# The first pair of attention in a kernel of attention and two expert layers: an early table load, decay pieces on GpSimd, another order of query tiles, and gate weights read at attention's end

## The chip, the cores and the metric

One Trainium2 chip (trn2), one of its cores. The metric is the device time of one execution in microseconds (us), on the one core that runs. Five engines work side by side on a core: TensorE (PE in the rows, with its weight loads as PEld), VectorE (DVE), ScalarE (ACT), GpSimd (POOL) and SyncE (SP). SyncE here only issues transfers; the transfers themselves are carried by 16 DMA engines.

## What is computed

Three operators, one after the other, in float32.

```
attention   q, k, v: 4 x 8 heads x 576 x 64; f: 4 x 8 x 576
            cum    = cumsum(log(clip(f, 1e-4, 1)))
            scores = q k^T / 8 + cum_i - cum_j, causal
            out    = softmax(scores) v
layer 1     x = out as 2304 x 512
            y = (silu(x w_gate) * (x w_val)) w_out        inner width 1536
layer 2     one of 8 experts per row, by argmax(y w_gate) with softmax weight,
            times sigmoid(y w_output_gate); expert: relu(y w1) w2, inner width 1024
```

## The kernel before

**Attention** (class `Attention`) goes through 16 pairs of heads. In a pair the two heads (a = 0, 1) lie in the two halves of the 128 partitions. The 576 queries are cut into five tiles: tile 0 with 64 queries, tiles 1 to 4 with 128 each. `qk(p, i)` makes the scores of tile i of pair p: per head one product q·k into a PSUM tile `ps_s` (four buffers), and one that adds the decay. For tile 4, 576 keys wide, this is done in two halves. VectorE reduces each PSUM tile to its row minimum (L151), ScalarE takes the exponential (L159) into the tiles `e`. The decay term of pair 0 comes from the float32 sums `c8` directly; for the later pairs the sums are split into three bf16 pieces (`decay`, L93 to L96), written to memory (`cd`, L97) and read back as the rows `dk` (L116).

`tr(p, g)` transposes the exponentials on TensorE in four groups g (L175 for the first, L190 and others for the rest); ScalarE and VectorE copy them out of PSUM. `av` multiplies them with v. The row sums are inverted on VectorE (`rb`, L212 and L213), transposed on TensorE (`rt`, L219), copied by ScalarE (L221), written to memory as ten rows of 512 bytes (`rd`, L224) and read back broadcast to 128 partitions x 576 (`rb`, L226). `xout` multiplies the result with that broadcast on GpSimd (L235) and splits it into `xth` and `xtl` (L237, L238). `run` interleaves: the scores of pair p + 1 are made between the transposes of pair p. TensorE's order there is the order of the code (`manual_schedule`); the other engines' order is set by a scheduler, with `issue_after` as a constraint on it. An engine works through its list strictly in order, and so does SP with the transfers.

**SP's queue** carries all these transfers: per pair rd, rb, the load `qk` of pair p + 3 (L108), from pair 2 on in every second pair a weight load for layer 1 (`raw`, L314), the rows `dk` and the load `v` (L113). The constants `cst` (L886, 128 x 474) come once, in pair 1.

**At the start** come f (twice, into both halves), q and k of pair 0, the mask, the identity, v and the next q and k, and, issued by the scheduler ahead of their place in the code, the two gate weights `wg` and `wo` (`Route.gates`, L441, 128 x 4 x 8 each), which VectorE splits into `gw` (L443, L444). The routing uses `gw` while the last sixth of layer 1 runs. `warm` runs matmuls on zeros (`e0[0]`) ahead of the first product.

**Layer 1** (class `MoE1`): `gv` makes two products per step into PSUM tiles `ps_g` (three buffers), each with 12 matmuls (L377). ScalarE takes tanh of the first (L381), VectorE makes `hs` of it (L382, which reads the first product a last time, and L383, the second's), ScalarE and VectorE split it (L384, L385). So a buffer of `ps_g` comes free only when VectorE's L382 or L383 is done. The first matmul of layer 1 stands within pair 15.

Of the kernel before, what the change touches and what calls it, by code (L numbers as in the profile page):

```python
# [9 lines left out]
F32 = mybir.dt.float32  # L10
# [3 lines left out]
ACTF = mybir.ActivationFunctionType  # L14
# [25 lines left out]
class Attention:  # L40
# [32 lines left out]
    def decay_load(self, pool):  # L73
        nc = self.nc
        t = {nm: pool.tile([128, 1024], F32, tag="w", name="dec_" + nm)[:, :S] for nm in ("ft", "cum", "c8")}
        t["pc"] = pool.tile([128, 1024], F32, tag="w", name="dec_pc").bitcast(BF16)[:B * H, :3 * S]
        for a in (0, 64):
            nc.sync.dma_start(out=t["ft"][a:a + B * H], in_=self.io["f"])
            nc.vector.memset(t["ft"][a + B * H:a + 64], 1.0)
        nc.vector.memset(t["c8"], 1.0)  # L80
        return t.values()

    def decay(self, ft, cum, c8, pc):
        nc = self.nc
        pc = pc.rearrange("p (r s) -> p r s", r=3)
        nc.vector.tensor_scalar(ft, ft, 0.0001, 1.0, op0=ALU.max, op1=ALU.min)
        nc.scalar.activation(ft, ft, ACTF.Ln)
        nc.vector.tensor_tensor_scan(cum, c8, ft, 0.0, op0=ALU.mult, op1=ALU.add)
        nc.scalar.activation(ft[:1, :1], ft[:1, :1], ACTF.Exp)
        nc.vector.tensor_scalar_mul(c8, cum, 8.0)  # L90
        self.c8 = c8
        cum, c8 = cum[:B * H], c8[:B * H]
        nc.vector.tensor_copy(pc[:, 0], c8)  # L93
        nc.vector.tensor_sub(cum, c8, pc[:, 0])
        nc.vector.tensor_copy(pc[:, 1], cum)
        nc.vector.tensor_sub(pc[:, 2], cum, pc[:, 1])  # L96
        nc.sync.dma_start(out=self.cd, in_=pc)  # L97

    def warm(self, n):
        z = self.e0[0]  # L100
        tp = self.ps_t.tile([128, 512], F32, name="ps_t")
        for i in range(n):
            self.nc.tensor.matmul(tp[:, :128], z, z, start=True, stop=True)
# [136 lines left out]
    def run(self, extra, pool):  # L240
        dec = self.decay_load(pool)
        self.load(0)
        self.cst.load()
        self.decay(*dec)
        self.vload(0)
        self.load(1)
        self.rows(1)
        with self.tc.issue_after(self.mark[2].ins):
            self.vload(1)
        with self.tc.manual_schedule(engines={PE}):  # L250
            self.warm(WARM0)
            for i in (2, 3, 4, 1, 0):
                self.qk(0, i)
            for p in range(NP):
                with self.tc.issue_after(self.mark[2].ins):
                    if p + 2 < NP:
                        self.load(p + 2)
                    extra[0](p)
                nx = p + 1 < NP
                self.rb(p)  # L260
                exps = None
                for g, qs in enumerate(((2, 3), (4,), (1, 0), ())):
                    self.tr(p, g)
                    if g == 0:
                        self.rt(p)
                    elif g < 3:
                        extra[g](p)
                    if exps:
                        with self.tc.issue_after(self.mark[0].ins):
                            exps()  # L270
                        exps = None
                    if 0 < g < 3:
                        self.av(p, g - 1)
                    if nx:
                        for i in qs:
                            exps = self.qk(p + 1, i, i == 4)
                for g in range(2, 4):
                    self.av(p, g)
                if p + 2 < NP:
                    self.rows(p + 2)  # L280
                    self.vload(p + 2)
                self.xout(p)
# [129 lines left out]
GI = 3  # L412
WARM = (14, 3, 3, 3)
P0, P1 = 1, 1
H0, WARM0 = 2, 10
HALF = (2, 4, 5, 7, 8, 10)


# [475 lines left out]
def tile_kernel(tc, io, out, dbg=None):  # L894
    nc = tc.nc
    with ExitStack() as ctx:
        pool = lambda cx, nm, b=1, **k: cx.enter_context(tc.tile_pool(name=nm, bufs=b, **k))
# [6 lines left out]
        with ExitStack() as c1:  # L904
            xp = pool(c1, "x")
            xth = xp.tile([128, 4, N], F32R, name="xth")
            xtl = xp.tile([128, 4, N], F32R, name="xtl")
            raw = pool(c1, "raw", 2)
            tmp = pool(c1, "dtmp", 1)
            m1 = MoE1(tc, c1, cst, io, wts, raw, tmp, xth, xtl)  # L910
            with ExitStack() as ca:
                cst.attention(pool(ca, "acst"))
                at = Attention(tc, ca, cst, io, xth, xtl)

                todo = []

                def early(p):
                    if p == 1:
                        cst.rest()
                    if p == H0:  # L920
                        todo.extend(m1.parts(0))
                    if p >= H0 and (p - H0) % 2 == 0 and todo:
                        todo[0] = m1.fetch(todo[0][0]), *todo[0][1:]

                dec = []

                def late(p):
                    if p > H0 and (p - H0) % 2 and todo:
                        dec.append(m1.decode(*todo.pop(0), eng=nc.gpsimd))
                        with tc.issue_after(at.mark[0].ins), tc.issue_after(at.mark[1].ins):  # L930
                            next(dec[0])

                def last(p):
                    with tc.issue_after(at.mark[0].ins), tc.issue_after(at.mark[1].ins):
                        if p == H0:
                            cst.split()
                        if dec:
                            for _ in dec.pop():
                                pass

                at.run((early, late, last), wts.pools[0])
            m1.open(c1)
            wab = [wts.pools[0], pool(c1, "wB", 6)]
            slp = pool(c1, "slots", space=PSUM)
            slots = slp.tile([128, 512], F32, name="slots")
            rt = Route(tc, c1, cst, io, per, m1.y)
            rt.gates(pool(c1, "gtmp"))
            CH = [(384 * i, 384) for i in range(6)]
            CL = CH[:4] + [(1536 + 256 * i, 256) for i in range(3)]
            steps = [(g, t0, n) for g in range(6) for t0, n in (CL if g == 5 else CH)]  # L950
            for i in range(len(steps) + 1):
                for f in range(2):
                    if i < len(steps):
                        g, t0, n = steps[i]
                        if g < 5 and t0 == 0 and f == 0:
                            wts.pools = [wab[(g + 1) % 2]]
                            if g:
                                m1.load(g + 1)
                        if i == 1 and f == 0:
                            wts.pools = [wab[1]]  # L960
                            todo.extend(m1.parts(1))
                        if 2 * i + f in HALF:
                            src, hi, lo = todo.pop(0)
                            with tc.issue_after(m1.mark[0].ins), tc.issue_after(m1.mark[1].ins):
                                for _ in m1.decode(m1.fetch(src), hi, lo):
                                    pass
                        if g == 5 and t0 == CH[2][0] and f == 0:
                            wts.pools = [wab[0]]
                            w00 = load_expert(nc, io, wts, raw, 0, 0)
                        m1.gv(g, t0, n, f)  # L970
                    if i:
                        for d in (2 * f, 2 * f + 1):
                            m1.g2(*steps[i - 1], d)
                if i and steps[i - 1][0] == 5:
                    rt.chunk(*steps[i - 1][1:], slots)
            info = rt.finish(slots)
# [89 lines left out]
```

## Time and profile before

| | |
|---|---|
| median of 3 runs | 969.86 us (968.68 to 972.22) |
| the profiled execution | 974.25 us, span 972.4 us |
| TensorE busy | 939.2 us, 97% of the span |
| VectorE, ScalarE, GpSimd busy | 592.1, 412.3, 228.8 us |
| TensorE's mean granted clock | 0.985 |
| attention | the first 209 us of the span |

The span runs from the first instruction to the last; the time of the execution also holds what lies around it. A row of the timeline has the start in us, the duration in us, the engine, the line of the code, the operation, what it writes and reads with the shape, how many instructions the row merges, and in brackets how long the engine was idle before it and what ended that. The granted clock is a share of full speed: 1.00 is 2.4 GHz and 0.50 is 1.2 GHz.

### The profile page before, as it was taken

To read this page: it belongs to the slowest core of one execution; us is meant where nothing else is said; L and a number is where in the kernel's file an instruction comes from. 1 tells how busy PE (TensorE), PEld (TensorE's weight loads), DVE (VectorE), ACT (ScalarE), POOL (GpSimd) and SP (SyncE) were. 2 spreads that over 40 slices of the span, in tenths; PEclk is the share of its full clock that TensorE was granted. 3 is DMA by queue.
4 is the path that set the end of the run, shared out by engine and by line. 5 is a ranking of instruction groups with operands and counts; after the bars stand their busy time and mean duration, and the time that the engine had idled before them with its cause. 6 is when DMAs were issued, how large, how long until landed. Compare 5 with 4: busy or idle time off the path is not lost.

```text
span 972.4 us, 16496 instructions
## 1 busy us (share of the span) xinstructions
PE 939.2 (97%) x6288; PEld 844.3 (87%) x6288; DVE 592.1 (61%) x1420; ACT 412.3 (42%) x903; POOL 228.8 (24%) x205
## 2 busy tenths in 40 slices
PE   8999999799999999999999999999899999999896
PEld 5666565479999999999999999899799999999795
DVE  5677776547487469459458445677785555552731
ACT  5677776534452123123123122333365445542741
POOL 1244444343121011012012000000115354372011
PEclk8999999999999999999999999999799999999998
DMA  5344444322132012013002000111486566582220
GB/s 161 115 134 132 132 131 127 109 66 66 44 109 65 1 45 86 1 32 100 1 22 87 1 1 1 43 56 55 156 284 191 170 217 188 197 296 85 73 91 30
DMA packets 53088, 94.83 MB, mean 98 GB/s; under 512 B 5954, under 2 KB 27086, under 8 KB 53007
## 3 DMA queue, kind: packets, MB, share of 16 engines
q1 hardware_dynamic: 47503, 79.58, 26.8%
q0 software_dynamic: 5504, 14.17, 4.1%
q8 instruction: 50, 0.82, 0.4%
q14 instruction: 31, 0.25, 0.1%
HBM read 84.10 MB, written 10.16 MB: 97 GB/s over the span
## 4 chain that ended last, share of the span: by engine, by line
PE 69%; issue 10%; DVE 8%; DMA 7%; POOL 3%; ACT 2%; SPq 1%; POOLq 0%; DVEq 0%; ACTq 0%
PE ps_g L377 26%; PE ps_y L395 13%; PE m_psy L696 7%; PE m_psg L681 7%; PE ps_s L144 5%; PE ps_t L190 3%; DMA rd<-rt 2%; DMA qk<-qk 2%; DVE dt L327 2%; PE avx L206 2%; PE avy L206 2%; DMA raw<-w 1%; POOL out L722 1%; PE rt_ps L532 1%; ACT e L159 1%
## 5 line engine op out<-in xcount | busy, mean ns | idle before, releaser
L377 PE MATMUL ps_g<-xth,w 128*128 128x384 f32 (+1 forms) x1184 | 308.7, 331 | 0.0
L377 PEld LDWEIGHTS ps_g<-xth,w 128*128 128x128 f32 x1184 | 213.1, 188 | 0.6
L377 PE MATMUL ps_g<-xtl,w 128*128 128x384 f32 (+1 forms) x592 | 196.1, 331 | 0.0
L395 PE MATMUL ps_y<-hh,w 128*128 128x384 f32 (+1 forms) x592 | 160.7, 332 | 2.2 <-DVE y L401 2.2
L681 PE MATMUL m_psg<-ygh,w 128*128 128x304 f32 x512 | 115.3, 307 | 1.2 <-ACT b_o L832 0.8
L696 PE MATMUL m_psy<-h2h,w 128*128 128x304 f32 x512 | 114.6, 306 | 0.0
L377 PEld LDWEIGHTS ps_g<-xtl,w 128*128 128x128 f32 x592 | 111.3, 188 | 0.1
L340 POOL TENSOR_TENSOR w<-ds,w 128x512 fp32r<-128x512 f32 x36 | 49.3, 1369 | 263.6 <-ACT w L339 263.2
L395 PEld LDWEIGHTS ps_y<-hh,w 128*128 128x128 f32 x592 | 107.1, 188 | 4.4 <-DVE y L401 4.1
L159 ACT ACTIVATE e<-e,mx 128x320 f32<-128x320 f32 (+4 forms) x160 | 88.0, 551 | 35.0 <-DVE mx L151 34.4
L608 DVE TENSOR_TENSOR w<-raw,w 128x1024 fp32r<-128x1024 f32 x64 | 76.7, 1222 | 40.8 <-ACT w L607 25.0
L395 PE MATMUL ps_y<-hl,w 128*128 128x384 f32 (+1 forms) x296 | 97.8, 330 | 0.0
L384 ACT ACTIVATE hh<-hs 128x384 fp32r<-128x384 f32 (+1 forms) x74 | 38.2, 516 | 134.4 <-DVE hs L383 134.4
L151 DVE CUSTOM_DVE_ANT_0 e<-ps_s,mask 128x320 f32<-128x320 f32 (+4 forms) x160 | 62.8, 429 | 47.4 <-PE ps_s L144 37.4
L382 DVE SCALAR_TENSOR_TENSOR hs<-hs,ps_g 128x384 f32<-128x384 f32 (+1 forms) x74 | 40.0, 541 | 83.4 <-ACT hs L381 83.4
L681 PEld LDWEIGHTS m_psg<-ygh,w 128*128 128x128 f32 x512 | 85.6, 189 | 1.8 <-ACT b_o L832 1.0
L696 PEld LDWEIGHTS m_psy<-h2h,w 128*128 128x128 f32 x512 | 85.5, 188 | 0.3
L607 ACT ACTIVATE w<-raw 128x1024 fp32r<-128x1024 f32 x64 | 67.4, 1058 | 36.4 <-PE m_psg L681 14.7
L381 ACT ACTIVATE hs<-ps_g 128x384 f32<-128x384 f32 (+1 forms) x74 | 35.5, 479 | 102.2 <-PE ps_g L377 102.1
L401 DVE TENSOR_TENSOR y<-ps_y,y 128x384 f32<-128x384 f32 (+1 forms) x124 | 67.1, 542 | 19.0 <-PE ps_y L395 18.2
L681 PE MATMUL m_psg<-ygl,w 128*128 128x304 f32 x256 | 77.3, 302 | 0.2 <-DVE ygl L649 0.2
L696 PE MATMUL m_psy<-h2l,w 128*128 128x304 f32 x256 | 77.3, 302 | 0.0
(309 smaller groups left out, 1511.6 us busy)
## 6 DMA issues: line engine op xcount, KB each, us to landing
raw<-w SPq DMA_DIRECT2D x64, 512.0 KB
qk<-qk SPq DMA_DIRECT2D x16, 576.0 KB
v<-vL SPq DMA_DIRECT2D x16, 448.0 KB
raw<-mg SPq DMA_DIRECT2D x12, 512.0 KB
raw<-mv SPq DMA_DIRECT2D x12, 512.0 KB
raw<-mo SPq DMA_DIRECT2D x12, 512.0 KB
rb<-rd SPq DMA_DIRECT2D x16, 288.0 KB
yd<-yr SPq DMA_DIRECT2D x18, 256.0 KB
```

The source lines that it names most:

```text
L144: nc.tensor.matmul(ps[a][b:, :n], x, y, start=c == 0, stop=c == 1, tile_position=(h, b))
L151: nc.vector.tensor_tensor_reduce(out=o, in0=x, in1=y, scale=-0.125, scalar=BIGF if prev[a] is None else prev[a][b:], op0=ALU.add, op1=ALU. ...
L159: nc.scalar.activation(es[a][b:, :w], es[a][b:, :w], ACTF.Exp, bias=prev[a][b:], scale=-1.0, accum_out=rs[b:, c:c + 1])
L340: nc.gpsimd.tensor_sub(lo, s3, hi.bitcast(F32))
L377: nc.tensor.matmul(ps[:, :n], w[:, k, fs], x[:, k], start=(k == 0 and c == 0), stop=(k == 3 and c == 2))
L382: nc.vector.scalar_tensor_tensor(s[:, :n], s[:, :n], 1.0, pss[0][:, :n], op0=ALU.add, op1=ALU.mult)
L395: nc.tensor.matmul(ps[:, :n], w[:, f, ds], h[:, f, :n], start=(f == 0 and c == 0), stop=(f == 1 and c == 2))
L401: nc.vector.tensor_add(y, ps[:, :n], y)
L607: nc.scalar.activation(hi, r, ACTF.Copy)
L608: nc.vector.tensor_sub(lo, r, hi.bitcast(F32))
L681: nc.tensor.matmul(ps[:, :C], w[:, k, fs], x[:, k], start=(k == 0 and c == 0), stop=(k == 3 and c == 2))
L696: nc.tensor.matmul(self.P[e][d][:, :C], w[:, f, ds], h[:, f], start=(u == 0 and f == 0 and c == 0), stop=(u == 3 and f == 1 and c == 2))
```

## The change

Five edits. The decay's table load: a one-element `Ln` on a tile of ones stands ahead of everything, so that ScalarE's table load precedes an instruction without a load from memory as its input. The four instructions that make the bf16 pieces go from VectorE to GpSimd. The order of pair 0's query tiles is 3, 4, 2, 1, 0 instead of 2, 3, 4, 1, 0, three matmuls on zeros (`WARM1`) follow them, and `warm` uses `e0[2]` instead of `e0[0]`. For pair 0, `rb` and `rt` stand behind the first two score tiles of pair 1 instead of around its first transposes. The gate weights' reads may be issued only after the last transposes' copy (`mark[1]`) and the last broadcast read (`mark[2]`) of attention.

```diff
@@ decay_load
         t = {nm: pool.tile([128, 1024], F32, tag="w", name="dec_" + nm)[:, :S] for nm in ("ft", "cum", "c8")}
+        one = self.sm.tile([128, 1], F32, name="one")
+        nc.vector.memset(one, 1.0)
+        nc.scalar.activation(one, one, ACTF.Ln)
@@ decay
-        nc.vector.tensor_copy(pc[:, 0], c8)
-        nc.vector.tensor_sub(cum, c8, pc[:, 0])
-        nc.vector.tensor_copy(pc[:, 1], cum)
-        nc.vector.tensor_sub(pc[:, 2], cum, pc[:, 1])
+        nc.gpsimd.tensor_copy(pc[:, 0], c8)
+        nc.gpsimd.tensor_sub(cum, c8, pc[:, 0])
+        nc.gpsimd.tensor_copy(pc[:, 1], cum)
+        nc.gpsimd.tensor_sub(pc[:, 2], cum, pc[:, 1])
         nc.sync.dma_start(out=self.cd, in_=pc)
 
     def warm(self, n):
-        z = self.e0[0]
+        z = self.e0[2]
@@ run
             self.warm(WARM0)
-            for i in (2, 3, 4, 1, 0):
+            for i in (3, 4, 2, 1, 0):
                 self.qk(0, i)
+            self.warm(WARM1)
             for p in range(NP):
...
-                self.rb(p)
+                if p:
+                    self.rb(p)
                 exps = None
                 for g, qs in enumerate(((2, 3), (4,), (1, 0), ())):
                     self.tr(p, g)
-                    if g == 0:
+                    if g == 0 and p:
                         self.rt(p)
...
                         for i in qs:
                             exps = self.qk(p + 1, i, i == 4)
+                    if g + p == 0:
+                        self.rb(p)
+                        self.rt(p)
@@
-H0, WARM0 = 2, 10
+H0, WARM0, WARM1 = 2, 10, 3
@@ tile_kernel
-            rt.gates(pool(c1, "gtmp"))
+            with tc.issue_after(at.mark[1].ins), tc.issue_after(at.mark[2].ins):
+                rt.gates(pool(c1, "gtmp"))
```

The change adds nine lines, so its line numbers are 3 to 9 higher than those of before.

VectorE in the first pair, before: from the scaled decay sums (`dec_c`) to the reduction of the second query tile. `ISA` is the reduction L151; its second row reads the minimum out.

```order
L90 TENSOR_SCALAR dec_c_153<-dec_cum 128x576
L93 CAST dec_pc<-dec_c_153 32x576
L94 TENSOR_TENSOR dec_cum<-dec_c_153,dec_pc 32x576
L151 ISA e,mx<-ps_s,mask 128x5x64
L151 ISA mx 128x1
L95 CAST dec_pc<-dec_cum 32x576
L96 TENSOR_TENSOR dec_pc<-dec_cum,dec_pc 32x576
L443 CAST gw<-gw_2862 128x4x16
L444 TENSOR_TENSOR gw<-gw_2862,gw 128x4x16
L151 ISA e,mx<-ps_s,mask 128x448
```

The same place of VectorE in the change.

```order
L93 TENSOR_SCALAR dec_c_153<-dec_cum 128x576
L154 ISA e,mx<-ps_s,mask 128x448
L154 ISA mx 128x1
L154 ISA e,mx<-ps_s,mask 128x288
L154 ISA e,mx<-ps_s,mask,mx 128x288
L154 ISA e,mx<-ps_s,mask 128x5x64
```

The pieces and the gate weights are gone from between the reductions, and tile 2 (128x5x64) comes after tiles 3 and 4.

SP at the end of attention, before: the writes rd and reads rb of pairs 14 and 15 (rd_97, rd_98) and the weight loads of layer 1.

```order
L224 DMA rd_97<-rt 10x128
L226 DMA rb<-rd_97 128x1x576
L224 DMA rd_98<-rt 10x128
L226 DMA rb<-rd_98 128x1x576
L314 DMA raw<-mv 128x2x512 x2
```

And in the change.

```order
L227 DMA rd_97<-rt 10x128
L229 DMA rb<-rd_97 128x1x576
L227 DMA rd_98<-rt 10x128
L229 DMA rb<-rd_98 128x1x576
L449 DMA gw_2869<-wg 128x4x8
L449 DMA gw_2869<-wo 128x4x8
L322 DMA raw<-mv 128x2x512 x2
```

The two gate reads stand directly behind the last broadcast.

VectorE at the same place, before: from the last copy of attention into layer 1.

```order
L196 COPY ath_2792<-ps_t 128x320
L234 COPY xt<-avy 128x256
L382 SCALAR_TENSOR_TENSOR hs<-hs,ps_g 128x384
L383 SCALAR_TENSOR_TENSOR hs<-hs,ps_g 128x384
L385 TENSOR_TENSOR hl<-hs,hh 128x384
```

And in the change.

```order
L199 COPY ath_2799<-ps_t 128x320
L237 COPY xt<-avy 128x256
L451 CAST gw<-gw_2869 128x4x16
L452 TENSOR_TENSOR gw<-gw_2869,gw 128x4x16
L390 SCALAR_TENSOR_TENSOR hs<-hs,ps_g 128x384
L391 SCALAR_TENSOR_TENSOR hs<-hs,ps_g 128x384
L393 TENSOR_TENSOR hl<-hs,hh 128x384
```

The cast of the gate weights and its subtraction stand between attention's last copy and the first `hs` of layer 1.

## Rows read from the trace of the kernel before

**Rows 1.** Timeline of the first pair, VectorE, ScalarE and TensorE.

```profile
3.20 1.28 ACT L87 ACT_TABLE_LOAD   x1 [3.20 <-DMA dec_ft<-f]
3.24 0.46 DVE L86 TENSOR_SCALAR dec_ft<-dec_ft 128x576 f32<-128x576 f32 x1 [0.35 <-DMA dec_ft<-f]
...
4.49 0.68 ACT L87 ACTIVATE dec_ft<-dec_ft 128x576 f32<-128x576 f32 x1
...
6.60 0.46 DVE L90 TENSOR_SCALAR dec_c<-dec_cum 128x576 f32<-128x576 f32 x1
...
10.92 0.20 DVE L443 CAST gw<-gw 128x64 fp32r<-128x64 f32 x1 [0.74 <-DMA gw<-wo]
...
11.95 0.67 ACT L159 ACTIVATE e<-e,mx 128x448 f32<-128x448 f32 x1 [1.75 <-DVE mx L151]
...
16.09 0.88 PE L175 MATMUL ps_t<-cst,e 128*128 128x128 f32 x4 [1.19 <-ACT e L159]
...
17.87 0.37 PE L219 MATMUL avy<-cst,rr 128*32 128x128 f32 x1 [0.90 <-DVE rr L213]
...
18.17 1.44 PE L144 MATMUL ps_s<-qk 64*128 64x320 f32 x4
...
21.67 1.97 PE L190 MATMUL ps_t<-cst,e 128*128 128x128 f32 x8
```

**Rows 2.** Windows, TensorE: stretch, length, PE busy (instructions), granted clock, DMA share, GB/s.

```profile
17.30:24.10 6.80, 6.23 (x29) 0.50 0.38 97
...
187.50:190.10 2.60, 0.00 (x0) 1.00 0.12 46
191.40:194.80 3.40, 3.40 (x18) 0.50 0.44 114
```

**Rows 3.** Timeline of SP: start, duration of the issue, line, transfer.

```profile
10.21 0.33 SPq L97 DMA_DIRECT2D cd<-dec_pc  x1
12.09 0.34 SPq L116 DMA_DIRECT2D dk<-cd  x1
...
19.80 0.65 SPq L226 DMA_DIRECT2D rb<-rd  x1
...
33.04 0.30 SPq L224 DMA_DIRECT2D rd<-rt  x1
35.02 0.53 SPq L226 DMA_DIRECT2D rb<-rd  x1
...
48.27 0.51 SPq L226 DMA_DIRECT2D rb<-rd  x1
...
60.00 0.51 SPq L226 DMA_DIRECT2D rb<-rd  x1
...
203.76 0.30 SPq L224 DMA_DIRECT2D rd<-rt  x1
211.23 0.51 SPq L226 DMA_DIRECT2D rb<-rd  x1
```

**Rows 4.** Waits of SP up to 222 us: in total, times, longest (us).

```profile
SPq L226 <- DMA rd<-rt: 119.6, 16, 11.6
```

**Rows 5.** Windows, TensorE, while rb(15) runs.

```profile
213.00:219.00 6.00, 6.00 (x36) 1.00 0.12 47
```

**Rows 6.** Instructions of lines L237 and L238 on GpSimd: ns min/median/max.

```profile
L237 POOL CAST xth<-xt x16: 657/664/1166, 33.7 to 221.3; 128x576 fp32r<-128x576 f32 x16
...
L238 POOL TENSOR_TENSOR xtl<-xt,xth x16: 1400/1409/1747, 34.4 to 222.4; 128x576 fp32r<-128x576 f32 x16
```

**Rows 7.** Timeline of the change-over from attention to layer 1.

```profile
209.40 0.42 DVE L234 COPY xt<-avy 128x256 f32<-128x256 f32 x1 [0.92 <-PE avy L206]
209.41 0.44 PE L377 MATMUL ps_g<-xtl,w 128*128 128x384 f32 x1
...
212.20 0.56 DVE L382 SCALAR_TENSOR_TENSOR hs<-hs,ps_g 128x384 f32<-128x384 f32 x1 [2.38 <-ACT hs L381]
...
219.63 1.57 POOL L235 TENSOR_TENSOR xt<-xt,rb 128x576 f32<-128x576 f32 x1 [4.79 <-DVE hl L385]
```

## The prediction

> **What bounds the kernel now.** I read four views, in this order: the timeline of the first pair, the windows with TensorE's granted clock, SP's queue from the first pair to the end of attention, and the timeline of the change-over from attention to the first expert layer. The page's 97% for TensorE says that it bounds the kernel as a whole; it does not say that it bounds attention, and that is what this change needs.
>
> In the first pair the reader is to see three holes. ScalarE's load of the logarithm's table begins only when f has landed, at 3.20, and the logarithm starts at 4.49, although the clamp before it was done at 3.24 + 0.46 = 3.70. VectorE stands 0.74 us at 10.92 for the gate weights, which only the routing uses, and ScalarE, behind it, waits 1.75 us at 11.95 for a row minimum. And TensorE has finished its first transposes at 16.09 + 0.88 = 16.97, yet starts pair 1 at 18.17, because the small transpose L219 waits for VectorE's reciprocal at 17.87 [rows 1]. After these holes the clock falls: from 17.3 to 24.1 it is granted at 0.50, the lower of its two levels (1.2 GHz), and TensorE is busy for 6.23 us of that [rows 2].
>
> In SP's queue the reader is to see who paces the rest of attention. The broadcast rb(p) of pair p is issued when the small write rd(p) has landed. In the first pairs that takes 33.04 to 35.02, in the last 203.76 to 211.23: 7.5 us for ten rows of 512 bytes [rows 3]. All sixteen rb waits are put down to it, 119.6 us together [rows 4]. While rb(15) moves its 288 KB the DMA engines are busy by 0.12 of sixteen, that is about two of them [rows 5]. So rb runs on two engines, and whatever has a share on those two and is issued behind it lands behind it. This loop (rb, the loads behind it, rd, the next rb) takes 13.25 and 11.73 us for pairs 1 to 2 and 2 to 3 [rows 3]. From rb(1) on it, and not TensorE, sets when attention ends: near the end TensorE stands idle from 187.5 to 190.1 for a load that went out in this queue [rows 2].
>
> **The start.** Table load: its own instruction now has no data to wait for, so the logarithm starts at 3.7, a gain of 4.49 − 3.70 = 0.8 at the decay sums. The gate reads leave the start: VectorE loses the 0.74 wait, the 0.20 cast and a subtraction of about the same size. The four decay pieces leave VectorE too. Together they can take away no more than ScalarE's 1.75 us wait, so the last exponentials that the transposes need end earlier by 0.8 to 0.8 + 1.75 = 2.5 us. I take 1.5: tile 4, now second, needs two reductions per half before its exponentials can start, and part of the wait returns there. L219 is moved behind pair 1's first two tiles, which removes the 18.17 − 16.97 = 1.2 us. TensorE so starts pair 1 about 2.7 us earlier, at 15.5, and up to 6.23/2 = 3.1 more is gained if the clock stays at its upper level, which the three added matmuls and the missing holes make likely (70%).
>
> The decay pieces cost nothing: on GpSimd two casts at 0.66 and two subtractions at 1.41 [rows 6] make 4.1 us, from 7.06 − 0.8 = 6.3 [rows 1]; so their write leaves at about 10.8 instead of 10.21 and the read behind it 0.6 later than 12.09 [rows 3]; pair 1 needs them after 15.5. With GpSimd's longest rows (1.17 and 1.75) they would be 1.7 us later still, and still in time.
>
> How much of TensorE's 2.7 to 5.8 us reaches the end? Only what the loop of rb passes on. rb(0) is issued about when it was, 19.8: TensorE is 2.7 earlier, but L219 now stands behind two tiles of pair 1 (18.17 to 21.67 before, at half the clock; half of that, 1.8, at the full one) and its copy behind two exponentials. rb(1) came 35.02 − 19.80 = 15.22 after rb(0), since rd(1) was not ready before 33.04. With TensorE at least 2.0 earlier the loop alone decides: between 11.73 (nothing else in it) and 13.25 (a 512 KB weight load in it); here it carries a 237 KB load of constants, so I take the middle, 12.5. **Gain: 15.22 − 12.5 = 2.7 us**; ends 15.22 − 13.25 = 2.0 and 3.5, and 1.3 if rb(0) is late.
>
> **The end of attention.** The two gate reads now stand behind rb(15) on SP, and on VectorE the cast that waits for them stands right behind the copy of 209.40, ahead of the first layer's first hs [rows 7]. Nobody measured when they land there. The nearest row of a small transfer with nothing ahead is the decay write: 10.21 to 12.09, 1.9 us [rows 3]; issued at 211.23 + 0.51 and 0.5 later, the reads would land at about 214.1. If they have to wait out rb(15), they land just after it, and GpSimd, which waits for rb(15), starts at 219.63 [rows 7] (its row names VectorE's hl, which GpSimd does not read; rb is what it needs): about 219.9. I take the later value, because rd(15), also small and also issued right behind an rb, took 7.5 us and not 1.9.
>
> The Trainium skill's page "DMA: Bandwidth & Descriptors" (section "Queues, rings and completion order") says that each engine consumes its descriptors in ring order and that the completion count of a transfer lands only after that engine's earlier writes; its section "Why a DMA increments its semaphore by 16 and not by 1" says that a 128-partition transfer is spread over all 16 engines and one whose outermost count is 2 over the lowest two. By that rule the sum is the + 4.8 below, by the 1.9 us of a free transfer it would be − 2.7; the rows of rd agree with the rule, and how the gate reads are spread is shown by no row.
>
> What is queued behind the waiting cast: all of VectorE, and hs first, which frees the buffer of the first product. The layer has three such PSUM buffers, of 12 matmuls each; 36 matmuls take 6.0 us [rows 5], from 209.41 to 215.4 [rows 7], when TensorE needs the first buffer back. It gets it when the cast (219.9), the subtraction and hs (0.56) are through: 219.9 + 0.45 + 0.56 = 220.9. **Stall: 5.5 us** (5.2 to 5.8). After an idle stretch of 2.6 us the clock was granted at 0.50 for 3.4 us of work, a loss of 1.7; after the first pair's holes for 6.23, a loss of 3.1 [rows 2]. The new idle stretch is longer than the 2.6, so it falls here too; **2.0 us**, nearer to the first since TensorE then works on without holes. Nothing later takes this back: from here on TensorE is the bound, and the layer's weight loads are released by VectorE's own order and move with it. The order of the stall and of rb(15) is not changed by the gain at the start, since both sides of it move together.
>
> **Sum:** − 2.7 + 5.5 + 2.0 = + 4.8 us. The profiled execution took 974.25 us with a span of 972.4, some 4 us over the median of the runs shown; it should become 979.0. Against the median: 969.86 + 4.8 = **974.7 us**, 0.49% slower.
>
> **Rivals.**
> The gate reads come in time (17%). For it: they are 32 KB, and at the start they delayed VectorE by no more than 0.74 us although much larger loads were ahead of them. Against it: rd. They decide for the stall only if they land after about 214.4, when cast, subtraction and hs would end after 215.4. Then only the start remains: 969.86 − 2.7 = 967.2, faster than before.
> The start's gain is lost (13%): the clock falls in pair 1 as before and rd(0), now behind two tiles at half the clock, makes rb(0) 1.5 to 2.7 us later, so that the loop starts late. Gain 0.5 in place of 2.7: 976.9.
> The loop is not the bound (10%): TensorE's whole gain with the upper clock arrives, 5.8: 969.86 − 5.8 + 7.5 = 971.6. For it: TensorE does not wait for a load in the first hundred microseconds. Against it: the sixteen waits of rows 4.
>
> **The numbers.** The forecast has 60%, its own range 972 to 977.5: the gain between 1.3 and 3.5, the stall between 5.2 and 5.8, the clock's loss between 1 and 3.1. To leave out no more than 2 in 10 the range must reach to the first rival's 967 and to 978: it leaves out half of that rival (8%) and 8% at the other ends. About 0.5%, or 4.85 us, is what a measurement of this kernel can tell from no change. Slower by more: half of the forecast (30%) and most of the second rival (12%), 0.42. Faster by more needs the first rival with more than 4.85 gained: 0.06. Within: 0.52.
>
> **What would show it.** Right: the logarithm near 3.7; pair 1's first matmul near 15.5; rb(0) near 19.8 and rb(1) near 32.3; rb(15) and the end of attention about 2.7 earlier; then a VectorE wait of some 10 us put down to the gate reads, TensorE idle for about 5.5 us after its third product, and 0.50 granted behind it. Wrong: a cast of gw that starts within 3 us of its reads' issue; rb(1) later than 34; an end of attention that moves by 5 us or not at all.

## The result and the profile after

| | before | the change |
|---|---|---|
| median of 5 runs, us | 969.86 (968.11 to 972.22) | 982.09 (978.40 to 984.22) |
| ratio, with its 95% interval | | 1.0109 (1.0087 to 1.0131) |
| profiled execution, us (span) | 974.25 (972.4) | 978.41 (976.6) |
| first product of layer 1 after attention, us | 209.41 | 205.47 |
| TensorE's wait ahead of the fourth product, us | 0 | 7.94 |

The change is 1.1% slower. The forecast was 974.7 us in 967 to 978: the direction was right, the size too small, and the time lies outside the range. The two profiles lie only 4.2 us apart and the medians 12.2; the experiments come back to that difference.

The first pair after the change, in the timeline of VectorE, ScalarE, GpSimd and TensorE (start, duration, engine, line, operation):

```profile
3.79 0.68 ACT L90 ACTIVATE dec_ft<-dec_ft 128x576 f32<-128x576 f32 x1 [1.57 <-DVE dec_ft L89]
...
6.42 0.65 POOL L96 CAST dec_pc<-dec_c 32x576 bf16<-32x576 f32 x1 [3.29 <-DVE dec_c L93]
...
10.21 0.77 ACT L162 ACTIVATE e<-e,mx 128x576 f32<-128x576 f32 x1 [0.52 <-DVE mx L154]
...
13.41 0.88 PE L178 MATMUL ps_t<-cst,e 128*128 128x128 f32 x4 [0.25 <-ACT e L162]
...
14.22 0.81 PE L147 MATMUL ps_s<-qk 64*128 64x320 f32 x4
...
16.04 0.28 PE L222 MATMUL avy<-cst,rr 128*32 128x128 f32 x1
```

The holes of [rows 1] are smaller or gone: the logarithm starts at 3.79 in place of 4.49, ScalarE, once its exponentials have begun, waits 0.52 in place of 1.75, and pair 1 starts at 14.22 in place of 18.17. Its first matmuls take 0.81 us, not 1.44: the clock did not fall.

SP's queue in the timeline, against [rows 3]:

```profile
18.41 0.65 SPq L229 DMA_DIRECT2D rb<-rd  x1
...
31.04 0.53 SPq L229 DMA_DIRECT2D rb<-rd  x1
...
208.50 0.50 SPq L229 DMA_DIRECT2D rb<-rd  x1
209.06 0.48 SPq L449 DMA_DIRECT2D gw<-wg  x1
209.58 0.49 SPq L449 DMA_DIRECT2D gw<-wo  x1
```

And the change-over to layer 1, against [rows 7], in the timeline of GpSimd, VectorE and TensorE:

```profile
217.05 1.40 POOL L238 TENSOR_TENSOR xt<-xt,rb 128x576 f32<-128x576 f32 x1 [4.97 <-DMA rb<-rd]
217.33 1.16 DVE L451 CAST gw<-gw 128x64 fp32r<-128x64 f32 x1 [11.46 <-DMA gw<-wo]
218.51 0.66 POOL L240 CAST xth<-xt 128x576 fp32r<-128x576 f32 x1
218.53 0.72 DVE L452 TENSOR_TENSOR gw<-gw,gw 128x64 fp32r<-128x64 f32 x1
219.17 0.54 DVE L390 SCALAR_TENSOR_TENSOR hs<-hs,ps_g 128x384 f32<-128x384 f32 x1
219.25 1.41 POOL L241 TENSOR_TENSOR xtl<-xt,xth 128x576 fp32r<-128x576 f32 x1
219.77 0.69 PE L385 MATMUL ps_g<-xth,w 128*128 128x384 f32 x1 [7.94 <-DVE hs L390]
```

The gate reads leave 0.56 and 1.08 us behind rb(15) and are there only after it: GpSimd, which waits for rb(15), starts at 217.05, VectorE's cast at 217.33. VectorE has stood for 11.46 us, and `hs`, which frees the first product's buffer, stands behind it. TensorE did its three products and then nothing from 211.83 to 219.77. In the windows behind it (stretch, length, busy time of PE, PEld, DVE, ACT, POOL, granted clock, DMA share, GB/s) the clock has fallen to its lower level (0.5, 1.2 GHz) for 3.3 us, a loss of 1.6:

```profile
211.50:219.70 8.20, 0.33 (x2) 0.01 (x1) 2.33 (x3) 0.00 (x0) 3.09 (x4) 0.78 0.11 30
219.70:223.00 3.30, 3.23 (x10) 3.23 (x11) 1.59 (x4) 0.90 (x2) 0.96 (x1) 0.51 0.00 0
223.00:228.00 5.00, 5.00 (x31) 5.00 (x30) 3.68 (x7) 1.58 (x3) 0.00 (x0) 1.00 0.00 0
```

### The profile page after: what moved, and what is told of

It is laid out like the page before. It is cut to its first block, busy times and chain, and to the rows that moved or that the text cites. A ratio compares the mean times of both kernels' runs of the same rounds, so it can differ in the third digit from the quotient of the medians.

```text
span 976.6 us, 16510 instructions
## 1 busy us (share of the span) xinstructions
PE 936.3 (96%) x6294; PEld 844.5 (86%) x6294; DVE 590.5 (60%) x1417; ACT 411.7 (42%) x904; POOL 232.7 (24%) x209
## 4 chain that ended last, share of the span: by engine, by line
PE 66%; DMA 11%; issue 10%; DVE 7%; POOL 2%; ACT 2%; SPq 0%; POOLq 0%; DVEq 0%; ACTq 0%
PE ps_g L385 25%; PE ps_y L403 13%; PE m_psy L704 7%; PE m_psg L689 6%; PE ps_s L147 5%; DMA rd<-rt 4%; DMA qk<-qk 3%; PE ps_t L193 2%; DVE dt L335 2%; PE avy L209 2%; PE avx L209 1%; DMA dk<-cd 1%; DMA raw<-w 1%; POOL out L730 1%; PE rt_ps L540 1%
## 5 line engine op out<-in xcount | busy, mean ns | idle before, releaser
L403 PE MATMUL ps_y<-hh,w 128*128 128x384 f32 (+1 forms) x592 | 160.8, 333 | 2.2 <-DVE y L409 2.2
L403 PEld LDWEIGHTS ps_y<-hh,w 128*128 128x128 f32 x592 | 107.1, 188 | 4.2 <-DVE y L409 4.0
L162 ACT ACTIVATE e<-e,mx 128x448 f32<-128x448 f32 (+4 forms) x160 | 88.0, 551 | 34.2 <-DVE mx L154 33.8
L403 PE MATMUL ps_y<-hl,w 128*128 128x384 f32 (+1 forms) x296 | 98.0, 331 | 0.0
L154 DVE CUSTOM_DVE_ANT_0 e<-ps_s,mask 128x448 f32<-128x448 f32 (+4 forms) x160 | 62.6, 429 | 46.3 <-PE ps_s L147 37.4
```

Source lines behind the costliest of these rows:

```text
L154: nc.vector.tensor_tensor_reduce(out=o, in0=x, in1=y, scale=-0.125, scalar=BIGF if prev[a] is None else prev[a][b:], op0=ALU.add, op1=ALU. ...
L162: nc.scalar.activation(es[a][b:, :w], es[a][b:, :w], ACTF.Exp, bias=prev[a][b:], scale=-1.0, accum_out=rs[b:, c:c + 1])
L403: nc.tensor.matmul(ps[:, :n], w[:, f, ds], h[:, f, :n], start=(f == 0 and c == 0), stop=(f == 1 and c == 2))
```

## The experiments

**Theory A:** the time is lost at the end of attention, where VectorE's cast waits for reads that stand behind a transfer on two DMA engines. **Rival B:** the edits of the first pair cost it. **Rival C:** the reads are slow by themselves. **Rival D** (of the run with rb in two): rb is bound by its bytes. **Rival E:** the last rows of attention are late, whatever the cast does. The runs fell on chips of two speeds, on which the kernel before takes 969.8 and 983 to 985 us; so only ratios to the kernel before on the same chip are compared, and times inside attention and layer 1. There the chips agree: from the first product to the last matmul of layer 1 the kernel before takes 478.99 us in its first profile, on the faster chip, and 478.95 in two on the slower.

**The change again, and one part undone or done alone.** `again` is the changed kernel. `gates_back` undoes the gate edit, `gates_only` does it alone in the kernel before:

```
 gates_back (in the changed kernel), gates_only has the reverse
-            with tc.issue_after(at.mark[1].ins), tc.issue_after(at.mark[2].ins):
-                rt.gates(pool(c1, "gtmp"))
+            rt.gates(pool(c1, "gtmp"))
```

> The changed kernel once more, unaltered, for a second profile. Theory A (the time is made at the end of attention: the gate reads stand behind rb(15), which runs on two DMA engines, and VectorE and TensorE wait for them) expects the ratio to stay near 1.01, the cast of gw some 8 to 9 us after its reads' issue, TensorE idle 7 to 9 us ahead of its fourth product, and, where this run is slower than the first profile's 978.4, the difference either in that idle stretch or in stretches at the lower clock. Rival B (the edits of the first pair cost the time, the first profile having been a lucky one) expects pair 1's first matmul, rb(0) or rb(1) later than 14.2, 18.4 and 31.0 in a slower run.

> The changed kernel with the gate reads back at their old place at the start; everything else of the change stays. Theory A expects the stall and the cold stretch behind it gone and the gain of the start left: rb(15) 2 to 3 us earlier than the 211.2 of before, the first product of layer 1 some 4 us earlier than 209.4, nothing idle ahead of the fourth product, ratio 0.994 to 0.998 (964 to 968). Rival B expects a ratio of 1.003 or more.

> The kernel before with the gate reads alone moved to the end of attention. Theory A: rb(15) near 211.2, reads behind it, cast of gw near 220 and, if it is as slow as in the changed kernel (1.2 us, with a subtraction of 0.7), the fourth product at 222.3 in place of 215.4: stall 6.9 and 1.5 at the lower clock, together +8.4, ratio 1.007 to 1.010. Rival B expects 1.000 to 1.004. Rival C (the reads are slow by themselves: 1024 rows of 32 bytes) gives the same time here and is told apart by the run with rb in two parts.

Measured: 1.0098 (1.0068 to 1.0129) for the change again, **1.0016 (0.9996 to 1.0036) with the reads back, 1.0108 (1.0074 to 1.0141) with the reads moved alone**. The gate edit makes all of the slowdown, and rival B falls. Timeline of the kernel with the reads moved alone:

```profile
215.37 1.17 DVE L443 CAST gw<-gw 128x64 fp32r<-128x64 f32 x1 [11.64 <-DMA gw<-wo]
...
217.80 0.69 PE L377 MATMUL ps_g<-xth,w 128*128 128x384 f32 x1 [8.14 <-DVE hs L382]
```

But the other edits do not gain their 2 to 4 us either, and the expectation for `gates_back` missed. Timeline of that kernel, VectorE and SP in the first pair:

```profile
11.41 0.20 DVE L451 CAST gw<-gw 128x64 fp32r<-128x64 f32 x1 [1.60 <-DMA gw<-wo]
11.64 0.23 DVE L452 TENSOR_TENSOR gw<-gw,gw 128x64 fp32r<-128x64 f32 x1
...
20.53 0.65 SPq L229 DMA_DIRECT2D rb<-rd  x1
...
33.18 0.53 SPq L229 DMA_DIRECT2D rb<-rd  x1
```

A first pair that is faster up to there only waits longer for the same reads: 1.60 us, not 0.74, in front of a reduction of the second tile. Then pair 1 starts at 16.35, rb(0) leaves at 20.53 and rb(1) at 33.18. With the reads gone and nothing else changed (`gates_only`) pair 1 starts at 16.82, later than that, and yet rb(0) leaves at 18.45 and rb(1) at 30.83, as in the full change. Timeline of that kernel, TensorE and SP in the first pair:

```profile
16.82 0.81 PE L144 MATMUL ps_s<-qk 64*128 64x320 f32 x4
...
18.45 0.65 SPq L226 DMA_DIRECT2D rb<-rd  x1
...
30.83 0.53 SPq L226 DMA_DIRECT2D rb<-rd  x1
```

In these profiles the earlier table, the GpSimd pieces and the order of tiles moved TensorE but not the loop of rb: the small transpose L222, put behind two tiles of pair 1, held back rb(0). That the removal of the reads brought rb(0) and rb(1) forward is not shown by them: each is one execution, and the kernel before, unaltered, has rb(1) anywhere from 31.52 to 35.02 (the last table below).

**The transfer.** `rb_two`, in the changed kernel:

```
-        self.mark[2] = nc.sync.dma_start(out=rb, in_=d.unsqueeze(1).to_broadcast([2, 64, S]))
+        for a in range(2):
+            self.mark[2] = nc.sync.dma_start(out=rb[64 * a:64 * a + 64], in_=d[a:a + 1].to_broadcast([64, S]))
```

> The changed kernel with the broadcast rb in two transfers of 64 partitions each in place of one of 2 x 64, so that its outermost count no longer holds it on two DMA engines. Theory A: the broadcast takes about 2 to 3 us in place of 7; the gate reads land about 2 us after their issue and the stall is 1 us or less; the loop of rb is no longer what paces attention, so the waits for rd fall from 7.5 to about 2 us a pair, and the end of attention is earlier by what TensorE stood idle for loads (3 us or more). Time 958 to 966, ratio 0.988 to 0.996. Rival C (gate reads slow by themselves): the stall stays at 5 us or more although rb is short. Rival D (the broadcast is bound by its 288 KB, not by its engines): rb still takes 7 us and nothing changes against the changed kernel.

Measured: **0.9877 (0.9847 to 0.9908)**, 958.3 us where the kernel before took 969.8. SP's waits for rd (in total, times, longest, us):

```profile
SPq L230 <- DMA rd<-rt: 33.5, 16, 3.6
```

SP's timeline at the end of attention:

```profile
186.64 0.31 SPq L227 DMA_DIRECT2D rd<-rt  x1
187.94 1.09 SPq L230 DMA_DIRECT2D rb<-rd  x2
189.07 0.59 SPq L450 DMA_DIRECT2D gw<-wg  x1
189.71 0.51 SPq L450 DMA_DIRECT2D gw<-wo  x1
```

VectorE's timeline there:

```profile
193.53 0.93 DVE L452 CAST gw<-gw 128x64 fp32r<-128x64 f32 x1 [0.83 <-DMA gw<-wo]
```

And two windows, with the columns as above:

```profile
120.00:190.00 70.00, 70.00 (x612) 43.53 (x610) 50.31 (x191) 49.85 (x152) 35.47 (x31) 1.00 0.40 126
190.00:230.00 40.00, 40.00 (x243) 39.23 (x242) 21.30 (x37) 13.85 (x28) 7.39 (x6) 1.00 0.16 44
```

The same reads, issued as closely behind rb(15), keep VectorE for 0.83 us in place of 11.46, and TensorE for none. Two things make up the 10.6 us: the cast starts 5.59 us after rb(15)'s issue and no longer 8.83, and rb(15) now leaves 4.8 us ahead of the end of VectorE's last copy (192.70) instead of 2.6 behind it (205.87). Rival C falls as the cause of the stall, but not altogether: with rb short the cast still starts 3.8 us after the issue of the second read, where it took 7.8. The sixteen waits for rd are 33.5 us, against 136.2 in the change and 119.6 in the kernel before [rows 4], though rb moves the same bytes: rival D falls. TensorE has no hole left from 120 to 230, rb(15) leaves 20.6 us earlier than in the change, and the loop of rb no longer paces attention. The Trainium skill, "DMA: Bandwidth & Descriptors", "Why a DMA increments its semaphore by 16 and not by 1", says that a transfer is spread over the largest number of engines, up to 16, that divides the outermost counts of its source and its destination. This run agrees: 2 x 64 became 64 twice, and nothing else. In the window from 178.6 to 182.0, where rb(14) alone moves, the 16 engines are busy by 0.24 and move 87 GB/s, against the 0.12 and 47 GB/s of [rows 5].

**The cast.** `cast_late` leaves the reads where the change put them and moves VectorE's two instructions, the cast and the subtraction of gw, out of `gates` into `gsplit`. The call of it, cut out of the edit:

```
+                if i == 4:
+                    with tc.issue_after(m1.mark[0].ins), tc.issue_after(m1.mark[1].ins):
+                        rt.gsplit()
```

> The changed kernel with the gate reads where the change put them, but VectorE's cast and subtraction of gw some forty instructions later, in the fourth step of layer 1. Theory A (it is the waiting cast at the head of VectorE that costs, not the reads) expects no idle time of TensorE ahead of the fourth product, and from the change only the earlier start: 965 to 970, ratio 0.995 to 1.000. Rival E (what is late is the end of attention itself, whose last rows need rb(15) on GpSimd): TensorE still idles several us, in the step that needs xth and xtl of pair 15, ratio 1.005 or more.

Measured: **0.998 (0.9951 to 1.0009)**, 983.6 us where the kernel before took 984.8. Its windows over the change-over:

```profile
207.00:213.00 6.00, 6.00 (x38) 5.93 (x38) 1.90 (x4) 1.46 (x3) 2.35 (x3) 1.00 0.11 33
213.00:219.00 6.00, 6.00 (x37) 6.00 (x36) 3.47 (x8) 2.08 (x4) 1.80 (x2) 1.00 0.17 44
219.00:225.00 6.00, 6.00 (x37) 6.00 (x36) 3.96 (x4) 1.95 (x5) 5.11 (x4) 1.00 0.29 87
```

And the cast in VectorE's timeline:

```profile
252.63 0.19 DVE L455 CAST gw<-gw 128x64 fp32r<-128x64 f32 x1
```

The reads are late and harm nobody; TensorE works through at 1.00. What costs is a waiting instruction at the head of VectorE's queue. Rival E falls: rb(15) left at 210.58 here, even later.

**The edits where rb is short.** rb in two in the kernel before, in `gates_only`, in the change with the late cast, and in `gates_back`:

> The kernel before with rb in two transfers of 64 partitions and nothing else. The theory that the loop of rb paces attention in the kernel before expects 8 us or more less than before: with the loop gone the first pair's holes and its stretch at the lower clock count in full, so 4 to 7 us more than the changed kernel with rb in two: 962 to 966, ratio 0.992 to 0.996. If TensorE paced the attention of before, it is the same as before within 2 us.

> The kernel before with the gate reads at the end and rb in two; beside the changed kernel with rb in two (958.3) it lacks the other three edits of the first pair (table load, GpSimd pieces, order of tiles and the late small transpose). The theory that these edits do work in the first pair and are swallowed by the loop of rb expects them to be worth, with the loop gone, what pair 1 starts earlier by: 16.8 - 14.2 = 2.6 us, so 960 to 962. If they are worth nothing anywhere: 958 to 959.

> The changed kernel with rb in two and the late cast of gw. With rb short the cast in its old place is no longer waited for long (0.83 us of VectorE's time in the profile of rb in two), so both theories expect no more than 1 us less than rb in two: 957 to 959, ratio 0.987 to 0.989. If it is 3 us or more better, the late cast is worth something also without the stall.

> The changed kernel with rb in two and the gate reads back at the start. VectorE then waits for them in the first pair (1.6 us and 0.4 of work in the run with the reads back alone), and with the loop of rb gone that should cost its 2.0 us in full: ratio about 0.990 where rb in two with the reads at the end had 0.9877. If the reads' place is worth nothing once rb is short, 0.987 to 0.988.

| with rb in two | ratio | pair 1's first matmul | last matmul of layer 1, us |
|---|---|---|---|
| kernel before | 0.9903 (0.9869 to 0.9937) | 17.41 | 677.07 |
| gate reads moved alone | 0.9878 (0.9845 to 0.9912) | 16.88 | 675.38 |
| all edits but the gate reads | 0.9896 (0.9858 to 0.9933) | 15.23 | 672.09 |
| all edits | 0.9877 (0.9847 to 0.9908) | 14.35 | 671.17 |
| all edits, late cast | 0.986 (0.9824 to 0.9897) | 14.21 | 671.02 |

The last column is the start of the last matmul of layer 1's second product (L395 in the kernel before, moved by a few lines in the others). rb alone brings 1.0% to the kernel before, more than expected: its loop paced attention. In the profiles, one of each kernel, the four other edits are worth 675.38 − 671.17 = 4.2 us here and the reads' removal 0.9 to 1.7; the timed runs cannot tell these from nothing, since all five intervals overlap. Part of the 4.2 is the clock: from 17 to 24 us it was granted at 0.76 in the profile with the gate reads moved alone, and at 1.00 in that with all edits. The kernel with the gate reads moved alone was expected to take 2.6 us more than that with all edits; the profiles have such a difference, the times do not show it. All edits with rb in two, with or without the late cast, beat both kernels.

**Why the profiles lie 4 us apart and the medians 12.** Three more profiles:

> The kernel before, unaltered, for a second profile. The first profile took 974.25, above all timed runs (968 to 972). If that one was at the slow end of a spread that comes from the loop of rb, this profile shows other TensorE holes and stretches at the lower clock in attention (the first had them at 17 to 24 and at 191 to 195), rb(15) a few us away from 211.2, and the stages after attention as long as in the first.

> As the run ahead of it, a third profile of the kernel before: the end of attention (first product of layer 1 at 209.4 in the first profile) is expected anywhere from 203 to 210, and the layer behind it without an idle stretch.

> The changed kernel for a third profile. Expected whatever attention does: cast of gw 8 to 9 us after its reads' issue, TensorE idle 7 to 9 us ahead of the fourth product and 0.50 granted behind it. Set against the two profiles of the kernel before on the same chip the end of layer 1 should be 5 to 12 us later, in place of the 4 to 6 of the first pair of profiles.

| profile | rb(1) | first product of layer 1 | rb(15) behind it | wait of TensorE ahead of the fourth product | first matmul of the second product (L395/L403) |
|---|---|---|---|---|---|
| before, first | 35.02 | 209.41 | 1.82 | 0 | 221.83 |
| before, second | 33.43 | 207.25 | 3.59 | 0 | 219.67 |
| before, third | 31.52 | 204.32 | 3.55 | 0 | 216.74 |
| the change, first | 31.04 | 205.47 | 3.03 | 7.94 | 227.55 |
| the change, second | 30.79 | 204.87 | 2.47 | 6.88 | 226.72 |
| the change, third | 31.79 | 205.76 | 3.45 | 7.93 | 228.94 |

One kernel's attention ends anywhere within 5 us, and within 2.9 in its second and third profile, both on one chip. The profile that the prediction was read from was the latest of three. Part of that is in its first pair; the window from 17 to 24 us of the second profile of before:

```profile
17.00:24.00 7.00, 6.71 (x42) 3.43 (x42) 3.36 (x13) 3.66 (x11) 0.00 (x0) 0.76 0.45 121
```

The third:

```profile
17.00:24.00 7.00, 7.00 (x57) 4.11 (x57) 5.02 (x18) 4.53 (x15) 0.00 (x0) 1.00 0.50 127
```

The 0.50 of [rows 2] is one execution's: the next has 0.76 and the third 1.00, so the holes of the first pair do not always bring the clock down. Of the six profiles with the first pair's old order four have less than 1.00 in this window; all eight with the new order have 1.00. In the mean of three the first product comes 1.6 us earlier by the change (207.0 to 205.4), not 3.9. From it to the first L395 or L403 the kernel before takes 12.42 us each time, the change 22.08, 21.85 and 23.18: +9.4 to +10.8. Together that is some 8 us, the lower end of what the timed runs show (1.0087, or 8.4 us). The 2 us that are missing to the middle of the interval, 1.0109, stay open; with three profiles of each kernel and a spread of 5 us in one of them they are no contradiction.

The first pair of profiles shows less, for two reasons. There the first product comes 3.9 us earlier, from 209.41 to 205.47, and the last matmul of layer 1 5.6 later, from 688.40 to 693.97. And from there to the end of the span, which is layer 2 and touched by no edit, the one took 284.0 us and the other 282.6, which leaves 4.2. In the six profiles on the faster chip this stretch takes 282.6 to 286.1, in the eight on the slower 296 to 306.

## Why the prediction was wrong in size and right in kind

**Right.** The logarithm at 3.79 (3.7 foretold). Pair 1 at 14.22, better than 15.5, with the clock kept. The loop of rb as the bound of attention: 12.63 us from rb(0) to rb(1) (12.5 foretold), though rb(0) left at 18.41 and not at 19.8; the run with rb in two confirms the mechanism. The decay pieces at no cost: their write left at 10.52 (10.8 foretold). The reads behind rb(15): the cast began 217.33 − 208.50 = 8.83 us after rb(15)'s issue, 219.9 − 211.23 = 8.67 foretold; the free transfer of 1.9 us, the rival with 17%, did not occur. The clock behind the stall: 1.6 us in the first profile (2.0 foretold, in 1 to 3.1), 2.6 and 2.8 in the other two.

**The step that failed first** is the gain, "15.22 − 12.5 = 2.7 us". In the pair of first profiles it holds to the digit at rb(15), from 211.23 to 208.50, but by luck: rb(1) came 4.0 us earlier (35.02 to 31.04), 1.4 of that because rb(0) did, and 1.3 were lost again on the way to rb(15). And the 15.22 belonged to an execution with a slow first pair; in the other two profiles rb(1) came 1.6 and 3.5 us earlier without any change. In the mean the gain at the first product is 1.6. The text said that the execution stood 4 us over the median and carried that offset through the sum as a constant; it was no constant, it sat in the very stage that the gain was taken from. Which edits carry the 1.6 stays open. With the reads at the start the others bring nothing (1.0016); with the reads moved they bring nothing that the times can tell (1.0108 without them, 1.0098 with them). What the profiles do show is that the new order kept the clock at 1.00 in every execution, where the old one lost it in some. The rival "the start's gain is lost" was nearer to the measured gain than the forecast, though for another reason: the clock did not fall.

**The step that failed second** is the stall of 5.5 us, which was 7.94, 6.88 and 7.93. Two things were mis-sized in it. rb(15) left 1.82 us after the first product in the profile read, and 2.5 to 3.6 after it in the five others, about 1.2 more in the first profile of the change. That "both sides of it move together" holds in the mean, with 2.99 us before and 2.98 in the change; it was again the one execution that stood apart. And cast and subtraction, priced at 0.45 together from their 0.20 at the start, took 1.16 and 0.72, 1.4 more. 5.5 + 1.2 + 1.4 = 8.1 against 7.94.

In the mean of the profiles + 4.8 should have been − 1.6 + 7.6 + 2.4 = + 8.4, with the stall as the largest part of the miss, or 978.3 us. That is the upper end of the range, and 4 us under the median of 982.09, 2 under the 980.4 that the ratio of 1.0109 makes of 969.86; where that rest is made no run shows. The range's upper end was set by the bounds of each term in one execution; that executions differ by more than these bounds was left out of it.

## What to carry to other kernels

A small read that nobody needs for long is free only if no engine queue waits for it: move the instruction that consumes it, not only the transfer (here 1.0098 with the cast in front of `hs`, 0.998 with it later). Before a transfer is put behind another, ask how many DMA engines the one ahead runs on; here the shape of one broadcast was worth more than every edit of the change. And where a stage waits on DMA, take the terms of a sum from several executions: here one profile lay anywhere in a spread of 5 us.

## What was unexpected of the hardware

The cast of gw, 64 elements in each partition, took 0.20 us at the start [rows 1] and 0.19 at 252.63 with GpSimd idle, but 1.16 beside GpSimd's multiplication (217.05 + 1.40 = 218.45; the cast ended at 218.49), and the subtraction 0.72 beside GpSimd's cast in place of 0.23. It ended, each time, within 0.1 us of GpSimd's instruction. The Trainium skill, "SBUF — State Buffer", "SBUF: two separate sides", says that the port pair that VectorE and GpSimd share is locked for a whole instruction and the other engine blocks, where VectorE's instruction runs in a mode with two ports or has two SBUF inputs. These rows agree for a cast from SBUF to SBUF and for a subtraction with two SBUF inputs; in which mode the cast ran no row shows. What makes the loop of rb vary from run to run was not tried, and stays open.
